# A three-stage kernel: the first chunk's scores from unspread blocks, a wake product, and a divided ordering of the experts

## The chip, the core and the metric

The kernel runs on one core of one Trainium2 chip. A core has TensorE (matrix products, PE in the rows), VectorE (DVE), ScalarE (ACT), GpSimd (POOL) and SyncE (SP, which here issues the loads), and 16 DMA engines that they share. The metric is the device time of the core in microseconds, the median of the runs.

## The reference

```python
q, k, a_re, a_im: [4, 8, 768, 48];  v the same;  all float32

for t in range(768):                                   # per batch and head
    ar, ai = normalised a_re, a_im at t                # a * min(|a|, 0.999) / (|a| + 1e-6)
    S_re, S_im = ar*S_re - ai*S_im + k[t] (x) v[t],  ar*S_im + ai*S_re
    y[t] = q[t] @ S_re
x = y as [3072, 384]                                   # tokens x (heads * 48)
xn = x / rms(x) * rms_g
h = silu(xn @ w_gate) * (xn @ w_val)                   # 384 -> 1536
x = h @ w_out                                          # 1536 -> 384
e = argmax(x @ w_gate2);  p = softmax at e             # 8 experts
out = p * (max(x @ w1[e], 0) @ w2[e])                  # 384 -> 1024 -> 384
```

The scan over t is done in closed form by chunks of 128 tokens: with the running product of a written as magnitude times phase, a chunk's scores are products of q times that running product and k divided by it, and a state of 48 x 48 per head goes from chunk to chunk.

## The kernel before

**Tiling.** The 3072 tokens are 12 units of 256 (two chunks of 128 each). A unit goes through three stages. *Elementwise* (`elem`, L485 to L627): magnitude, running products, phase, cosine and sine on tiles of 128 x 768 (three blocks j of 128 rows, which are heads times 48, by 256 tokens), on ScalarE and VectorE; the results are `qk` (q and k times the cosine) and `ee` (q and k times the sine). Ten DMAs then *spread* them (L625) from 128 rows, where a head of 48 lies across blocks, to `QK`, 96 rows (48 of cosine, 48 of sine) for each of 8 heads. *Attention* (`chunk`, L649): scores k q (L680), transposed k (L698), products with v (L720, and L724 with the state), transposition of the new state (L747) and of the rows (L765), norm, and transposition of the normed row y to x (L805). *Dense* (`feature`, L838): twelve features of 128 columns; the products into both gates (L850, 18 of 256 columns, split into high and low parts), tanh and products on ScalarE and VectorE, the rounding `hh` and its remainder `hl` (L867), and the output products (L873). The experts come last (`expert`, L1242): products L1299, rounding `ehh` and remainder `ehl` (L1308), products L1317.

**Weights.** The dense weights come as bfloat16 halves and are put together in the start (`convert`, L381): a memset on GpSimd, `top` (L395), `join` (L401), `high` (L408), and `low`, the remainder, which for two groups (`w000`, `wo00`) is made by products on TensorE (L430 and L431). `logit_columns` (L441) multiplies the output weights with the gate of the experts, transposing them first (L450), then L460 and the transposition L466. An expert's two weight matrices are loaded in 3 pieces of 1024 columns and 4 of 768 (`load_weights`, L1073), through one staging buffer `rawa` for the first expert and three buffers `rawb` for the others; ScalarE converts each piece (L1095) and VectorE or GpSimd takes the remainder.

**The order.** Nothing is written in the order in which it runs. Every step is added to a plan with its engines, costs, readers and writers and a due time, and `issue` (L185) puts them out: the step that can start first, by the plan's costs, and of an engine's equals the one that is due first. Due times come from a table of numbers (`TUNE`, L34). Each engine runs its own list in that order, and waits by semaphores.

**Fillers.** `keep_warm` (L1388) is a step of eight products of 128 x 384, whose result nobody reads. Fifteen such steps are added with a due time of 1e6, the last of all, so `issue` takes one where TensorE by its plan would wait; after 107.43 us of the plan they are left out.

**Ordering of the experts.** Beside the last dense features, VectorE sorts the experts by their counts in tiny operations: `second` (L1004, 7 operations) and `sort` (L1015, 8 operations), one step of the plan each.

## Time and profile before

| | us |
|---|---|
| median of 3 runs (935.48 to 936.58) | 936.08 |
| the profiled execution | 936.97 |
| its span, first to last instruction | 935.3 |
| TensorE busy | 896.5 (96%) |
| VectorE busy | 613.2 (66%) |
| ScalarE busy | 518.0 (55%) |
| GpSimd busy | 181.6 (19%) |

The span is that of the profiled execution, 1.7 us shorter than its time; the rest lies around it. Busy times are sums of one engine's instructions, and engines overlap.

### The profile page before, as it was taken

How to read it: one execution, taken by the hardware profiler on the slowest of the kernel's cores; microseconds unless marked ns; L12 is line 12 of the kernel's file. 1: busy time of each engine (PE TensorE's matmuls, PEld its weight loads, DVE VectorE, ACT ScalarE, POOL GpSimd, SP SyncE). 2: the span in 40 equal slices, each digit the busy share in tenths (PEclk: the TensorE clock that was granted, in tenths of full speed). 3: DMA queues.
4: the chain of work that ended last, by engine and by line, in shares of the span. 5: the costliest groups of instructions: out<-in, count | busy, mean ns of one | idle time of the engine just before them, and what ended most of it. 6: DMA issues, size and time to landing. Idle time of an engine off the chain costs nothing.

```text
span 935.3 us, 17743 instructions
## 1 busy us (share of the span) xinstructions
PE 896.5 (96%) x6747; PEld 863.5 (92%) x6747; DVE 613.2 (66%) x1528; ACT 518.0 (55%) x996; POOL 181.6 (19%) x226
## 2 busy tenths in 40 slices
PE   2699999999999999999999999999999999999996
PEld 2689999999999999999999999999989989999996
DVE  5699867778777768686868777546566642545510
ACT  7787876675655656655656565424426433544421
POOL 3232302010111010110201020101242532222121
PEclk9899999999999999999999999999999999999999
DMA  9955233423333140605050421102346753545200
GB/s 331 292 196 140 65 78 82 102 83 77 95 61 94 45 127 18 154 18 154 17 137 19 92 80 40 48 1 66 93 122 200 219 144 111 151 129 182 91 23 23
DMA packets 68363, 98.12 MB, mean 105 GB/s; under 512 B 16038, under 2 KB 49257, under 8 KB 68276
## 3 DMA queue, kind: packets, MB, share of 16 engines
q1 hardware_dynamic: 57316, 86.61, 32.9%
q0 software_dynamic: 10688, 9.95, 3.9%
q8 instruction: 54, 0.88, 0.4%
q10 hardware_dynamic: 272, 0.40, 0.1%
q14 instruction: 33, 0.27, 0.1%
HBM read 68.19 MB, written 10.15 MB: 84 GB/s over the span
## 4 chain that ended last, share of the span: by engine, by line
PE 68%; DVE 11%; issue 8%; DMA 5%; ACT 5%; POOL 2%; SPq 0%; POOLq 0%; DVEq 0%; ACTq 0%
PE m L850 25%; PE a L873 15%; PE a L1317 7%; PE m L1299 7%; PE t L680 4%; PE t L720 3%; DVE ee L541 2%; PE t L724 1%; DMA out_dram<-eo,idx 1%; PE t L698 1%; POOL out_dram L1325 1%; DMA QK<-qk 1%; DMA rawb<-in_w_dram 1%; DVE re L576 1%; DVE rs L785 1%
## 5 line engine op out<-in xcount | busy, mean ns | idle before, releaser
L850 PE MATMUL m<-xh,w 128*128 128x256 f32 x1728 | 276.6, 285 | 1.1 <-DVE s L862 0.6
L850 PEld LDWEIGHTS m<-xh,w 128*128 128x128 f32 x1728 | 234.6, 188 | 5.7 <-issue 3.4
L873 PE MATMUL a<-wo,hh 128*128 128x392 f32 (+1 forms) x576 | 151.8, 345 | 0.0
L850 PE MATMUL m<-xl,w 128*128 128x256 f32 x864 | 149.1, 281 | 0.0
L850 PEld LDWEIGHTS m<-xl,w 128*128 128x128 f32 x864 | 122.3, 188 | 0.0
L873 PEld LDWEIGHTS a<-wo,hh 128*128 128x128 f32 x576 | 100.5, 188 | 0.7 <-issue 0.7
L873 PE MATMUL a<-wo,hl 128*128 128x392 f32 (+1 forms) x288 | 98.3, 341 | 1.7 <-DVE hl L867 1.7
L865 ACT ACTIVATE hh<-s 128x256 fp32r<-128x256 f32 x144 | 59.5, 415 | 72.9 <-PE a L873 45.7
L857 ACT ACTIVATE s<-m 128x256 f32<-128x256 f32 x144 | 54.6, 380 | 77.8 <-PE m L850 40.1
L867 DVE TENSOR_TENSOR hl<-s,hh 128x256 fp32r<-128x256 f32 x144 | 66.6, 467 | 29.4 <-ACT hh L865 28.7
L859 DVE SCALAR_TENSOR_TENSOR s<-s,m 128x256 f32<-128x256 f32 x144 | 59.4, 413 | 21.3 <-ACT s L857 21.1
L1325 POOL DMA_INDIRECT out_dram<-eo,idx x28 | 37.2, 1330 | 157.7 <-ACT eo L1323 91.2
L1308 DVE SCALAR_TENSOR_TENSOR ehl<-m,ehh 128x384 fp32r<-128x384 f32 (+6 forms) x64 | 35.2, 555 | 44.6 <-ACT ehh L1306 44.0
L862 DVE SCALAR_TENSOR_TENSOR s<-s,m 128x256 f32<-128x256 f32 x144 | 59.6, 415 | 2.1
L1323 ACT ACTIVATE eo<-a,eg 114x384 f32<-114x384 f32 (+5 forms) x28 | 16.3, 582 | 74.9 <-PE a L1317 60.6
L873 PEld LDWEIGHTS a<-wo,hl 128*128 128x128 f32 x288 | 54.1, 188 | 2.3 <-DVE hl L867 2.3
L1306 ACT ACTIVATE ehh<-m 128x384 fp32r<-128x384 f32 (+6 forms) x64 | 31.2, 491 | 44.8 <-PE m L1299 41.7
L720 PE MATMUL t<-AK,vt 128*64 128x224 f32 (+3 forms) x384 | 49.6, 346 | 0.5 <-ACT raw L465 0.3
L680 PE MATMUL t<-QK 96*128 96x128 f32 x384 | 48.1, 276 | 0.3 <-DMA QK<-ee 0.3
L680 PEld LDWEIGHTS t<-QK 96*128 96x128 f32 x384 | 46.3, 192 | 1.3 <-issue 0.8
L948 POOL DMA_INDIRECT slots<-tid,sl x24 | 25.0, 1043 | 115.7 <-DVE cnt L943 111.8
L690 DVE TENSOR_TENSOR AK<-t,mask 128x512 f32<-128x512 f32 x40 | 26.9, 686 | 21.3 <-PE t L680 21.1
...
## 6 DMA issues: line engine op xcount, KB each, us to landing
...
```

The costliest lines, as they stand in the source:

```text
L680: TE.matmul(sc.t[:, i, :], lhsT=K(4 * g + i), rhs=Q(4 * g + i), start=True, stop=True)
L720: TE.matmul(yt.t[64 * n:64 * n + d, i, :n_], lhsT=vs[:, o:o + d], rhs=ak.t[:, 2 * i + n, :n_], start=True, stop=first)
L850: TE.matmul(ps.t[:, i, :], lhsT=W1[i, g].t[:, k, part, fs], rhs=x.t[:, k, :], start=(n == 0), stop=(n == 3 * KD - 1))
L857: add((A, act(U)), lambda e: e.activation(s.t, ps.t[:, 0, :], AF.Tanh, scale=0.5), r=[ps], w=[s], due=dh, table=AF.Tanh)
L859: add((V, dve(U)), lambda e: e.scalar_tensor_tensor(out=s.t, in0=s.t, scalar=1.0, in1=ps.t[:, 0, :], op0=ALU.add, op1=ALU.mult), r=[s, ps] ...
L862: add((V, dve(U)), lambda e: e.scalar_tensor_tensor(out=s.t, in0=s.t, scalar=0.5, in1=ps.t[:, 1, :], op0=ALU.mult, op1=ALU.mult), r=[s, ps ...
L865: add((A, act(U)), lambda e: e.activation(hh.t, s.t, AF.Copy), r=[s], w=[hh], due=dh)
L867: lambda e: e.tensor_tensor(out=hl.t, in0=s.t, in1=hh.t, op=ALU.subtract), r=[s, hh], w=[hl], due=dh, lock=True)
L873: TE.matmul(acc[t].t[:, :wide], lhsT=h.t[:, ts_], rhs=WO[g].t[:, k3, part, :wide], start=(f == 0 and n == 0), stop=(f == KF - 1 and n == 2))
L1299: TE.matmul(ps.t, lhsT=w.t[:, k, fs], rhs=y.t[:, k, :], start=(i == 0), stop=(i == 3 * KD - 1))
L1317: TE.matmul(po.t, lhsT=h.t[:, f, js], rhs=w.t[:, f, :], start=(f == 0 and i == 0), stop=(f == KF2 - 1 and i == 2))
L1325: add((G, 1.05), lambda e, o=o, j=j: e.indirect_dma_start(out=outs[(x + j) % len(outs)], out_offset=bass.IndirectOffsetOnAxis(ap=at(j), ax ...
```

## The change

**Scores of the first chunk.** They are no longer computed from `QK`, but from `qk` and `ee` as they stand in 128 rows, ahead of the spread. A head of 48 rows can start only at certain rows of a product's operand; so where another head's rows are in the way, the k side is a copy in which those are zero (`own`, by the column `part`). That takes 20 products instead of 8, each pair for cosine and sine. `rows` is split in two: the half with the scores needs no `QK`, the half for the state does and gets a later due time (`KS`).

```diff
+        def bank(*shape, own=True):
+            return Buf(k_u if apart and own else k_t, shape=list(shape))
...
                 out=S2.t, in0=T.t, in1=gm.t.unsqueeze(2).to_broadcast([2 * D, H, D]), op=ALU.mult),
                r=[T, gm], w=[S2], lock=True)
...
+        def places(h):
+
+            if h < 6:
+                return [(h // 2, slice(0, D) if h % 2 == 0 else slice(0, 2 * D), h % 2)]
+            return [(2 * (h - 6), slice(2 * D, P), 0), (1, slice(2 * D, 112 if h == 6 else P), h - 6)]
+
...
+                        TE.matmul(sc.t[:, i, :], lhsT=K(h), rhs=Q(h), start=True, stop=True)
+                        continue
+                    ops = [(pair[n].t[rs, j, U:U + C] if not masked else own.t[rs, n, j], pair[n].t[rs, j, :C])
+                           for n in range(2) for j, rs, masked in places(h)]
+                    for n, (k_, q_) in enumerate(ops):
```

(The lines above are the places of heads 6 and 7 and the products; `pair` is `qk` and `ee`.)

**Elementwise of the first unit.** Each operation is cut into two halves of 384 elements (one for each chunk), and the arctangent moves ahead of the exponentials. The steps of the first unit are marked `first`; `foresee` works out when each could start, and `issue` takes no other step on an engine that would run past that by over 0.1 us (`RS`), TensorE left out.

```diff
+    def foresee(self, firsts):
+
+        for s in firsts:
+            e, c = s.engs[0][:2]
+            t = s.span[0]
+            for d in s.deps:
+                t = max(t, (d.end if d.end is not None else d.done if d.first else math.inf)
+                        + self.hop(d.eng if d.end is not None else d.engs[0][0], e))
+            s.soon, s.done = t, t + c + s.lag + s.size / 350e3
...
                 raise RuntimeError("no step can be issued")
+            if firsts:
+                taken = {}
+                for s in firsts:
+                    e = s.engs[0][0]
+                    if e is not self.pe:
+                        taken[e] = min(taken.get(e, math.inf), s.soon)
+                cand = [c for c in cand if c[1].first or c[3] <= taken.get(c[2], math.inf) + TUNE["RS"]] or cand
...
+        parts = range(NC) if u == 0 else [None]
+        NE_ = N3 // len(parts)
+
+        def at(*a, shift=0.0, **kw):
+            due[0] += 1.0 / len(parts)
+            return add(*a, due=due[0] + shift, pull=(TUNE["PE0"], TUNE["PE1"])[u] if u < 2 else 0.0, first=u == 0, **kw)
...
+        order = [(0, 0), (1, 0), (0, 1), (1, 1)]
+        for i, sin in order:
+            key, y = "pm"[i], angle if sin else ta
+            each(either, lambda e, c, i=i, sin=sin, y=y: e.tensor_tensor(
+                out=half(ee if sin else qk, i, c), in0=half(ee, i, c), in1=cut(y, c), op=ALU.mult),
+                r=[(ee, key), y], w=[(ee, key) if sin else (qk, "qk"[i])], lock=True, shift=sh)
+        state["whole"] = qk, ee
+        state["moves"] = [] if u == 0 else state["moves"]
```

**Weight conversions.** Loads from the fourth conversion on wait for the last spread DMA; `top` runs on ScalarE or GpSimd only; the memset waits for the loads.

**Wake and warm-up.** TensorE's first instruction becomes a product that reads the first half of the exponential; behind it stand nine steps of eight products of 128 x 128 (`FE`), to be taken as fillers are.

```diff
 
         for k in range(KD):
             dma(lambda e, k=k: e.dma_start(halves()[:, k, 1:1 + 4 * WB], src[k * P:(k + 1) * P]),
-                P * WB * 8, w=[(st, f"k{k}")], due=due, after=paces[-AHEAD:][:1] if len(paces) >= AHEAD else ())
+                P * WB * 8, w=[(st, f"k{k}")], due=due, after=(paces[-AHEAD:][:1] if len(paces) >= AHEAD else [])
+                + (state["moves"][-1:] if len(paces) >= TUNE["NB"] else []))
         light = [(A, act(N)), (G, 0.08 + N * 1.04e-3), (V, dve(N / 2), TUNE["RB"])]
         pairs = [(st, f"k{k}") for k in range(KD)]
-        add((G, 0.08 + N * 0.96e-3), lambda e: e.memset(raw.t, 0.0), w=[raw], due=due - 2, lock=True)
-        paces.append(add(light, top, r=pairs, w=[raw], due=due, lock=True))
+        add((G, 0.08 + N * 0.96e-3), lambda e: e.memset(raw.t, 0.0), r=pairs[:1] if len(paces) > 1 else [], w=[raw], due=due - 2)
+        paces.append(add([(A, 0.16 + N * 1.11e-3), (G, 0.16 + N * 1.13e-3)], top, r=pairs, w=[raw], due=due, lock=True))
...
+    def wake(ee):
+        add((TE, mm(P, 4)), lambda e: TE.matmul(fill.t[:, :P], lhsT=ident, rhs=ee.t[:, 0, U:U + C], start=True, stop=True),
+            r=[(ee, "m0")], w=[fill], due=-2000.0)
...
+        def warm_up(e):
+            for _ in range(8):
+                TE.matmul(fill.t[:, :P], lhsT=identr, rhs=identr, start=True, stop=True)
+
+        for _ in range(int(TUNE["FE"])):
+            add((TE, 8 * 0.1125), warm_up, r=[IDENTR, fill], w=[fill], due=1e6, span=(0.0, TUNE["W1"]))
```

**Experts.** The sort is cut into `sort`, `ranked` and `numbered`, one step each. `rawa` has three buffers of 392 columns instead of one of 1024. The first expert's pieces are 9 of 384 or 256 columns and 8 of 384 (instead of 3 and 4); the last 768-column piece of the others from the third on is cut in two, which go through `rawa`, and their loads are planned 6 us long instead of 2.

```diff
-    k_ra, k_rb = Slots(e_right, "rawa", [P, F2], F32), Slots(e_left, "rawb", [P, F2], F32, 3)
+    k_ra, k_rb = Slots(e_right, "rawa", [P, XW], F32, 3), Slots(e_left, "rawb", [P, F2], F32, 3)
...
+        def pieces():
+
+            for k in range(KD):
+                for lo, hi in ((0, F2),) if x else ((0, DM), (DM, 2 * DM), (2 * DM, F2)):
+                    yield 0, k, lo, hi, k
+            for f in range(0, KF2, 2):
+                for lo, hi in ((f, f + 2),) if x == 1 or x and f + 2 < KF2 else ((f, f + 1), (f + 1, f + 2)):
+                    yield 1, f // 2, lo, hi, f / 2 + 0.2 * (lo - f)
...
+            raw = Buf(k_rb if cols > DM else k_ra) if x else Buf(k_ra)
...
+            loads.setdefault(x, []).append(dma(load, P * cols * 4, w=[raw], due=due, after=after, lag=TUNE["DL"] if x < 2 else 6.0))
...
-                add((V, 1.3), second, r=[MORE, HOT], w=[PERM, SECOND], due=due_moe(u + 1, KF))
-                add((V, 2.0), sort, r=[MORE, HOT], w=[PERM], due=due_moe(u + 1, KF))
+                add((V, 1.1), second, r=[MORE, HOT], w=[PERM, SECOND], due=due_moe(u + 1, KF), lock=True)
+                for c, fn in ((0.6, sort), (0.72, ranked), (0.36, numbered)):
+                    add((V, c), fn, r=[MORE, HOT], w=[PERM], due=due_moe(u + 1, KF), lock=True)
```

Of the table of numbers 33 values change, and seven are new:

```diff
-            E3=785.18, CG=483.05, CO=263.88, LC=-203.35, NRAW=2, AHEAD=5, DH=547.2, FI=-16.42, RP=-1165.15, TOL=0,
+            E3=785.18, CG=-303.74, CO=-326.35, LC=-1082.81, NRAW=2, SH=169.53, NB=4, FE=9, RS=0.1, ATD=1, KS=-1056.86, PM=0.0, AHEAD=5, DH=547.2, FI=-16.42, RP=-1355.1, TOL=0,
```

**What moves in the lists.** TensorE's list at the head of the program, the last logit transposes (L450), a filler run and the first scores (L680) before:

```order
L450 MATMUL t_301<-identr,wo_268 128x128 x6
L450 MATMUL t_309<-identr,wo_268 128x128 x6
L450 MATMUL t_318<-identr,wo_268 128x128 x6
L1388 MATMUL a_244<-w_333,identr 128x384 x16
L680 MATMUL t_372<-QK_288 128x128 x4
L680 MATMUL t_384<-QK_288 128x128 x4
L698 MATMUL t_397<-ident,QK_288 128x96 x4
L698 MATMUL t_403<-ident,QK_288 128x96 x4
```

and of after (the scores are L805 there, the fillers and the warm-ups L1556 and L1560, the wake product L515):

```order
L1728 UNCONDITIONAL_BRANCH
L515 MATMUL a_227<-ee_197,ident 128x128
L1560 MATMUL a_227<-identr 128x128 x64
L805 MATMUL m_328<-qk_146 128x128
L805 MATMUL m_328<-ee_197 128x128
L805 MATMUL m_328<-qk_146,tb_302 128x128
L805 MATMUL m_328<-ee_197,tb_302 128x128
L805 MATMUL m_328<-qk_146 128x128
L805 MATMUL m_328<-ee_197 128x128
```

All weight products, logit transposes and fillers that stood ahead of the first scores now stand behind them.

TensorE's list inside the first unit's dense features (L850 before, L983 after; `w100` and the like are weight groups: first the matrix, 0 the gate's and 1 the value's, then which 384 of the 1536 columns), before:

```order
L850 MATMUL m2_716<-xh0_565,w100_333 128x256 x3
L850 MATMUL m2_716<-xl0_587,w100_333 128x256 x3
L850 MATMUL m2_716<-xh0_565,w100_333 128x256 x3
L1388 MATMUL a0_244<-w020_743,identr_64 128x384 x16
L850 MATMUL m0_780<-xh0_565,w010_527 128x256 x3
L850 MATMUL m0_780<-xl0_587,w010_527 128x256 x3
L850 MATMUL m0_780<-xh0_565,w010_527 128x256 x3
L850 MATMUL m0_780<-xh0_565,w110_421 128x256 x3
```

and after:

```order
L983 MATMUL m1_826<-xh0_537,w010_543 128x256 x3
L983 MATMUL m1_826<-xh0_537,w110_707 128x256 x3
L983 MATMUL m1_826<-xl0_549,w110_707 128x256 x3
L983 MATMUL m1_826<-xh0_537,w110_707 128x256 x3
L1556 MATMUL a0_227<-w010_543,identr_64 128x384 x16
L1556 MATMUL a0_227<-w110_707,identr_64 128x384 x16
L983 MATMUL m0_915<-xh0_537,w010_543 128x256 x3
L983 MATMUL m0_915<-xl0_549,w010_543 128x256 x3
```

Where one run of 16 fillers stood between two features, 32 stand now, one feature later.

VectorE's list at the ordering of the experts, beside the last dense features (`hl` is L867 before, L1000 after), before:

```order
L1013 TENSOR_SCALAR half1_78<-piece_76 128x1
L1020 SCALAR_TENSOR_TENSOR upto_73<-hot_67,nk_68 1x8
L1023 TENSOR_TENSOR grid_69<-upto_73 1x64
L1024 TENSOR_REDUCE rank8_75<-grid_69 1x8
L1025 TENSOR_TENSOR grid_69<-rank8_75,rev_95 1x64
L1026 TENSOR_TENSOR grid_69<-grid_69,rev_95 1x64
L1027 TENSOR_REDUCE perm_70<-grid_69 1x8
L1028 TENSOR_SCALAR perm_70<-perm_70 1x8
L1029 CAST permi_71<-perm_70 1x8
L867 TENSOR_TENSOR hl2_8543<-s0_8406,hh2_8507 128x256
L867 TENSOR_TENSOR hl0_8555<-s1_8444,hh0_8516 128x256
L867 TENSOR_TENSOR hl1_8565<-s2_8480,hh1_8529 128x256
```

and after:

```order
L1146 TENSOR_SCALAR half1_78<-piece_76 128x1
L1000 TENSOR_TENSOR hl2_8718<-s0_8617,hh2_8700 128x256
L1153 SCALAR_TENSOR_TENSOR upto_73<-hot_67,nk_68 1x8
L1155 TENSOR_TENSOR grid_69<-upto_73 1x64
L1156 TENSOR_REDUCE rank8_75<-grid_69 1x8
L1000 TENSOR_TENSOR hl0_8733<-s1_8649,hh0_8716 128x256
L1163 TENSOR_TENSOR grid_69<-rank8_75,rev_95 1x64
L1164 TENSOR_TENSOR grid_69<-grid_69,rev_95 1x64
L1165 TENSOR_REDUCE perm_70<-grid_69 1x8
L1000 TENSOR_TENSOR hl1_8744<-s2_8682,hh1_8731 128x256
L1170 TENSOR_SCALAR perm_70<-perm_70 1x8
L1171 CAST permi_71<-perm_70 1x8
```

The three `hl` that stood behind all of the ordering now stand between its parts.

## Rows read from the trace of the kernel before

**Rows 1.** stretches: us, busy us (x instructions) per engine, granted clock, DMA share, GB/s

```profile
0.00:66.44 66.44, 41.38 (x269) 35.16 (x270) 45.71 (x81) 51.64 (x74) 22.11 (x51) 0.95 0.88 288
...
86.88:650.00 563.12, 560.42 (x4668) 541.53 (x4668) 413.94 (x1124) 333.03 (x684) 74.97 (x106) 1.00 0.30 75
```

**Rows 2.** what TensorE waited for from 66.44 us on: us in total, times, longest

```profile
PE m L1299 <- DVE ehl L1308: 1.8, 1, 1.8
PE a L873 <- DVE hl L867: 1.7, 1, 1.7
```

**Rows 3.** stretches of the fillers alone (L1388), the third row around their slow run

```profile
0.00:66.44 66.44, 19.67 (x96) 18.00 (x96) 0.95 0.88 288
66.44:83.73 17.29, 4.64 (x25) 4.11 (x24) 1.00 0.29 92
...
34.00:40.00 6.00, 3.09 (x10) 3.09 (x11) 0.50 1.07 165
```

**Rows 4.** timeline: start, us, instruction, [idle before <- releaser]; ScalarE, then VectorE

```profile
13.80 1.49 ACT L395 ACTIVATE raw<-w 128x1152 f16<-128x1152 bf16 x1 [2.24 <-DMA w<-in_wg_dram]
...
27.86 1.83 DVE L608 TENSOR_TENSOR qk<-ee,ta 128x768 f32<-128x768 f32 x2 [1.50 <-ACT ta L597]
...
50.29 0.55 DVE L704 COPY AK<-t 128x384 f32<-128x384 f32 x1
```

**Rows 5.** timeline of SyncE's queue (SPq), which issues the loads and the spread

```profile
29.75 3.04 SPq L625 DMA_DIRECT2D QK<-qk  x3
```

**Rows 6.** timeline of TensorE, from the second group's weight products on

```profile
27.95 0.81 PE L430 MATMUL t<-raw,ident 128*128 128x384 f32 x2
...
29.58 2.12 PE L450 MATMUL t<-identr,wo 128*128 128x128 f32 x18
36.91 4.59 PE L1388 MATMUL a<-w,identr 128*128 128x384 f32 x16 [5.21 <-ACT w L406]
41.34 0.39 PE L680 MATMUL t<-QK 96*128 96x128 f32 x2
42.01 1.80 PE L680 MATMUL t<-QK 96*128 96x128 f32 x14 [0.28 <-DMA QK<-ee]
...
45.75 1.06 PE L680 MATMUL t<-QK 96*128 96x128 f32 x8
...
51.66 0.85 PE L460 MATMUL t<-raw,w2gt 128*32 128x128 f32 x18
...
60.42 0.25 PE L466 MATMUL t<-ident,raw 96*128 96x96 f32 x1
60.45 3.02 PE L1388 MATMUL a<-w,identr 128*128 128x384 f32 x16
63.31 0.49 PE L805 MATMUL t<-ident,y 128*128 128x128 f32 x3
...
66.44 0.52 PE L850 MATMUL m<-xh,w 128*128 128x256 f32 x3
```

**Rows 7.** timeline of VectorE (two middle subtractions), then of GpSimd (one conversion)

```profile
16.60 2.03 DVE L554 TENSOR_TENSOR ee<-ee 128x256 f32<-128x256 f32 x3
...
66.19 1.09 DVE L554 TENSOR_TENSOR ee<-ee 128x256 f32<-128x256 f32 x3
...
16.76 1.27 POOL L408 TENSOR_SCALAR w<-raw 128x1152 fp32r<-128x1152 f32 x1 [7.58 <-DVE raw L401]
```

**Rows 8.** timeline at the experts' ordering: VectorE, then TensorE

```profile
675.08 1.41 DVE L1006 SCALAR_TENSOR_TENSOR upto<-hot,nk 128x8 f32<-128x8 f32 x1
...
679.31 1.08 DVE L867 TENSOR_TENSOR hl<-s,hh 128x256 fp32r<-128x256 f32 x3
...
679.77 0.44 PE L873 MATMUL a<-wo,hl 128*128 128x392 f32 x1 [1.66 <-DVE hl L867]
```

**Rows 9.** timeline in the experts: ScalarE, then TensorE

```profile
767.61 0.84 ACT L1095 ACTIVATE h2b<-rawb 128x768 fp32r<-128x768 f32 x1 [4.40 <-DMA rawb<-in_w_dram]
...
770.04 0.92 PE L1299 MATMUL m<-exh,h1a 128*128 128x456 f32 x3 [1.82 <-DVE ehl L1308]
```

434 lines of the change are left out of this document (261 added, 173 removed).

## The prediction, made before the result was known

> **What bounds the kernel now.** I read the stretches first: up to 66.44 us, the start of the first dense product, TensorE is busy for 41.4 of 66.4 us; from 86.88 to 650 us for 560.4 of 563.1 [rows 1]. So the kernel is a start of 66 us followed by 860 us that are TensorE's own. The list of what TensorE waited for after the start says the same: 1.8 us and 1.7 us in one wait each, and 2.0 us in four small ones left out there [rows 2]. Two rules follow. Whatever brings the first dense product forward shortens the run one to one; whatever is put into TensorE's order behind that point lengthens it one to one, unless it stands where the engine would have waited. The filler products (x128x384, they compute nothing that is used) are the second kind: of 120, 96 stand ahead of 66.44 us and 24 behind [rows 3].
>
> **The start, what is ahead of the spread.** The order of work is a chain: exponentials and sine on ScalarE, products on VectorE, the spread of q and k into 96 rows by ten DMAs, then attention of two chunks, then the first dense product. Before, the two q products follow the cosine from 27.86 to 29.69 us, and the first spread is issued at 29.75 [rows 4, 5]. On ScalarE two weight conversions of 1.5 us stand ahead of the exponentials of the chain, one of them shown [rows 4]; of the four table loads of that stretch none is saved. The change moves the conversions behind the exponentials (one stays, where ScalarE waits for VectorE) and cuts every operation in two halves, so that the second half of one step lies beside the first half of the next. I walk the new order with the old durations: an operation of 768 elements starts the next one 0.75 us later on ScalarE and 0.87 on VectorE, one of 384 elements 0.40 and 0.45 (the 384-wide copy has 0.55 us from start to end [rows 4]). Logarithms end at 8.0, the exponential table at 9.3, the four halves of inverse and magnitude at 10.9, arctan with its table at 13.1, the table back at 14.35; VectorE's scans end at 13.35, middle subtraction of the first half 15.1, the exponentials 17.0; phase, turns and subtraction on VectorE 19.4, absolute value 19.8, sine table 21.05, first cosine half 21.7; then eight half products of 0.45, the sixth of which completes q and k: 24.5 us. The spread thus starts at 24.6 instead of 29.75, 5.1 us earlier.
>
> **The start, from the spread to the dense product.** The last piece landed 12.3 us after the first issue (42.01) [rows 5, 6]. The loads queued ahead fall from 28 of 384 KB to 18, so the queue is empty when the spread comes, and I take 11.2; the first four DMAs, three quarters of the bytes, serve heads 0 to 3 and should land at 24.6 + 8.3 = 32.9. TensorE gets there from the other side: the first exponential half of k is ready at 16.7, the wake product and 64 warm-ups at the lower and then the higher clock end near 25.6, the 20 direct score products at 0.25 each (four heads in 1.06, ends overlapping [rows 6]) near 30.6, three weight products 2.4 and the first rows 0.5: 33.5. Both ends meet there, so neither alone is the bound. Then TensorE's order up to the first dense product is a fixed list. Before, the like list ran from the first score at 41.34 to 66.44, 25.1 us [rows 6], with 56 fillers and 1.5 us of waits; the new one has 56 fillers too. It loses the waits, chunk 0's scores (2.0), the logit product and its transposition (0.85 and 0.25) and, by my estimate, 1.2 on rows that read 128 or 96 columns where they read 224; it gains three weight products (0.81 each, 2.4), the logit transposes (2.1) and eight warm-ups (0.9, as eight of those 18), which ran earlier or not at all [rows 6]: 24.7 us. The first dense product comes at 33.5 + 24.7 = 58.2, a gain of **8.2 us**. I walked ScalarE and VectorE too: they have its operands at 55.6. The clock is no term: the 1.2 GHz level was granted from 34 to 40 us (0.50) [rows 3], after 5.2 us in which TensorE stood idle, and it fell on fillers (16 in 4.59 [rows 6]). In the new order no such pause stands there.
>
> **What is put behind the dense start.** 64 fillers instead of 24 now stand there: 40 x 0.179 (16 take 2.86, from 60.45 to 63.31 [rows 6]) = **+7.2 us**. They are put where the planner saw TensorE wait for VectorE (a free accumulator, then the third weight group). By my walk they overshoot those waits by 1.7 and 2.2 us, so fillers, not VectorE, set the pace there. The first logit product and its transposition, before ahead of the dense start, come behind it: **+1.1 us** (nine products and one transposition [rows 6]). The twelve extra score products, the split rows and the masked copies of q and k lie ahead of 58 us and are in the sums above. So the whole start costs 7.2 + 1.1 - 8.2 = 0.1 us: the 8 us gained at the first dense product are handed back as filler.
>
> **The experts' ordering.** At 675.08 us VectorE runs 14 tiny operations in one piece, the first of them 1.41 us, and the three hl products that TensorE waits for come behind, at 679.31; TensorE stood idle 1.66 us [rows 8]. The change puts one hl behind each of three parts. After the first part (2.6 us) the first hl is done at 678.0, and TensorE was free at 678.1; each next one comes 1.1 us later, as long as TensorE takes for one hl. I take **-1.5 us** of 1.66, the ends being 0 and -1.66.
>
> **The last weight piece of an expert.** At 767.61 ScalarE had sat 4.4 us before a conversion whose load was late, and three ehh operations were queued behind it in its order; TensorE lost 1.82 us [rows 9]. Now the last two pieces of each expert from the third on have staging buffers of their own (free since the first expert), and the load is planned 6 instead of 2 us long. Ends 0 and -1.82; no later load stalled TensorE, so I take **-1.8**. The smaller pieces of the first expert (16 loads instead of 7) run where TensorE waits for nothing [rows 2] and cost nothing while that cover lasts; without it each is one more wait of the order of 0.5 us. The other waits (2.0 us in sum) I leave as they are.
>
> **Sum.** 0.1 - 1.5 - 1.8 = -3.2 us. The profiled execution took 936.97 us (span 935.3), so 933.8; the median 936.08 lies 0.9 below it, so **932.9 us**.
>
> **A rule that speaks against it.** VectorE's middle subtraction took 2.03 us with a GpSimd conversion running beside it (16.76 to 18.03) and 1.09 us without [rows 7]. The change gives GpSimd four more top conversions (1.5 us each, as on ScalarE [rows 4]) and three more high ones (1.27 [rows 7]) in the start, some 10 us more of such work beside VectorE operations that read two tiles. The Trainium skill, SBUF — State Buffer, section "Who interferes with whom", says that a VectorE instruction with two SBUF inputs contends with a GpSimd instruction that reads SBUF, and the loser blocks for the whole instruction. By that rule the trace's pair is as it should be, and the sum would lose what the fourth rival below loses.
>
> **Rivals.** (1) *More than that*: the walk has slack (operands at 55.6), the second and third hl wait nothing, and the 2.0 us of small waits go with the new order: 1.2 + 2.0 + 0.2 more, 929.5. For it: these waits hang on single placements [rows 2]. Against: any new order makes new ones. Chance 0.14. (2) *The stalls move*: the hl after the second part or another late load stops TensorE for as long as before: the sum is 0.1, 936.2. For it: VectorE is the engine that both waited for. Chance 0.14. (3) *The spread lands late*: heads 0 to 3 arrive only with the rest, as at 41 us before (first score at 41.34, but TensorE was busy with fillers up to then [rows 6], so the trace does not say); the list starts at 36.3, dense at 61, +2.8: 935.7. Chance 0.08. (4) *GpSimd blocks VectorE*, the one on the other side: 10 us of GpSimd work at up to its whole length, of which 3.9 us are covered by the filler overshoot. At 0.74 us lost per us (0.94 for 1.27 [rows 7]) 7.4 - 3.9 = +3.5, no change in sum; at the whole length +6.1, 939.0. It decides from 9.0 us lost: then the run is slower by over 0.2%. For it: rows 7. Against: the planner keeps most of these apart. Chance 0.12. The forecast itself has 0.52, from 931 to 934.2.
>
> **Chances and range.** A difference under 0.2% (1.9 us) can't be told from none here. Faster: forecast and (1), 0.66; same: (2) and (3), 0.22; slower 0.12. The dense start can be off by 1 to 4 us (57 to 62) and the two stalls by 3.3, so the range is 928.5 to 937.5; it leaves out most of (4) and the tail of (1).
>
> **What would show it.** The first spread issued near 24.6 us, the first dense product near 58, TensorE's granted clock never at its lower level after 22 us; 64 fillers behind the dense start with no wait longer than 0.3 us ahead of 88 us; no wait of TensorE for hl beside the ordering, none for ehl in the experts. If the first dense product comes after 61.5, or TensorE waits behind the fillers, the start is wrong; if the time falls by over 8 us, fillers were standing in waits that I took for work.

## The result, and the profile after

The changed kernel takes 950.24 us (median of 4 runs, 949.58 to 952.13) against 936.33 (935.48 to 938.17) for the kernel before beside it: a ratio of 1.0142, 95% interval 1.012 to 1.0164. It is slower by 13 to 14 us; 932.9 was predicted, with a range up to 937.5. The profiled execution took 949.58 us, 12.61 more than that of before.

Three points cut both kernels into the same three parts: the first dense product, the first product of the experts, and the end of the span. The first row is before, the last one is what the prediction's terms make of it.

| profiled execution | to the first dense product | dense stages | experts | span |
|---|---|---|---|---|
| before | 66.44 | 617.39 | 251.47 | 935.3 |
| after | 73.61 | 626.05 | 248.04 | 947.7 |
| difference | +7.17 | +8.66 | -3.43 | +12.4 |
| predicted | -8.2 | +6.8 | -1.8 | -3.2 |

(+6.8 is 7.2 of fillers, 1.1 of logit products, -1.5 of the ordering, which lies ahead of the experts' first product.) So the late part did better than predicted, the dense stages are 1.9 us worse, and the start is wrong by 15.4 us and in its sign.

The first view to read is the list of what TensorE waited for in the kernel after (us in total, times, longest):

```profile
PE a L515 <- POOL qk L655: 17.2, 1, 17.2
PE m L983 <- DVE s L995: 2.4, 3, 1.8
...
PE a L1006 <- DVE hl L1000: 0.6, 1, 0.6
```

The 17.2 us are the idle time ahead of its first instruction, the wake product. Behind that there are no 12 us of waits: TensorE was never idle for long, so the time must lie in how long its instructions take. The timeline of TensorE in the start of the kernel after (start, us, instruction, number):

```profile
17.19 0.77 PE L515 MATMUL a<-ee,ident 128*128 128x128 f32 x2 [17.19 <-POOL qk L655]
17.61 13.89 PE L1560 MATMUL a<-identr 128*128 128x128 f32 x64
31.43 0.79 PE L805 MATMUL m<-qk 48*128 48x128 f32 x2
...
42.04 1.65 PE L456 MATMUL t<-raw,ident 128*128 128x384 f32 x2
42.91 1.09 PE L457 MATMUL t<-w,x 128*128 128x384 f32 x1
...
46.11 0.75 PE L457 MATMUL t<-w,x 128*128 128x384 f32 x1
46.79 0.65 PE L847 MATMUL m<-AK,vt 128*64 128x128 f32 x8
...
49.69 1.09 PE L1560 MATMUL a<-identr 128*128 128x128 f32 x8
...
73.61 0.52 PE L983 MATMUL m<-xh,w 128*128 128x256 f32 x3
```

Compare the two L1560 rows: eight warm-ups take 1.09 us at 49.69 (0.14 each, pipelined ends included), and 64 of them take 13.89 us at 17.61 (0.217 each). The weight pair (L456 here, L430 in [rows 6]) takes 1.65 us where it took 0.81. Up to about 46 us TensorE ran at the lower of its two levels (1.2 GHz, against 2.4 at the upper one). The stretches of that time (us; busy us and instructions of PE, PE's weight loads, DVE, ACT, POOL; granted clock; DMA share; GB/s) do not say so:

```profile
17.19:31.43 14.24, 14.24 (x66) 14.12 (x66) 10.73 (x20) 8.36 (x13) 1.94 (x2) 1.00 0.58 177
31.43:42.04 10.61, 10.61 (x41) 9.04 (x41) 1.96 (x2) 1.16 (x1) 0.00 (x0) 1.00 0.88 237
42.04:46.79 4.75, 4.75 (x10) 2.82 (x9) 1.96 (x2) 0.49 (x1) 1.09 (x2) 1.00 1.05 387
```

The clock column (1.00 for the upper level, 0.50 for the lower) reads 1.00 in all three. It was the same in the kernel before, with 1.00 from 16.7 to 21 us although its first weight pair took twice as long as the third:

```profile
16.73 1.65 PE L430 MATMUL t<-raw,ident 128*128 128x384 f32 x2 [16.73 <-DVE raw L401]
...
20.01 0.81 PE L430 MATMUL t<-raw,ident 128*128 128x384 f32 x2
```

In these traces the column shows a fall that follows a rise [rows 3], not the level at which the program begins. That level is to be read from the duration of one and the same instruction at two places.

Elsewhere: GpSimd's conversion stood beside two VectorE operations as the fourth rival had it, the spread was issued at 26.59 instead of 24.6, and no wait for `hl` stands at the ordering nor one for `ehl` in the experts (a wait of 0.6 us for `hl` lies at 142.7 us, in another unit). SyncE's queue, VectorE and GpSimd of the kernel after:

```profile
26.59 1.40 SPq L719 DMA_DIRECT2D QK<-qk  x2
```

```profile
18.76 2.25 DVE L684 TENSOR_TENSOR im<-re,ta 128x384 f32<-128x384 f32 x2
18.86 1.81 POOL L422 TENSOR_SCALAR raw<-w 128x1152 f16<-128x1152 bf16 x1 [1.54 <-DMA w<-in_wv_dram]
```

### The profile page after: what moved, and what is told of

It is laid out like the page before. It is cut to its first block, busy times and chain, and to the rows that moved or that the text cites. A ratio compares the mean times of both kernels' runs of the same rounds, so it can differ in the third digit from the quotient of the medians.

```text
span 947.7 us, 18182 instructions
## 1 busy us (share of the span) xinstructions
PE 917.9 (97%) x6877; PEld 883.3 (93%) x6877; DVE 622.6 (66%) x1564; ACT 516.0 (54%) x1026; POOL 182.1 (19%) x234
## 4 chain that ended last, share of the span: by engine, by line
PE 71%; DVE 9%; issue 8%; ACT 5%; DMA 5%; POOL 1%; SPq 0%; POOLq 0%; DVEq 0%; ACTq 0%
PE m L983 24%; PE a L1006 14%; PE m L1465 8%; PE a L1483 7%; PE t L800 4%; PE t L847 3%; PE a L1560 2%; PE t L851 1%; DMA rawa<-in_w_dram 1%; DMA out_dram<-eo,idx 1%; DVE ee L600 1%; PE m L805 1%; PE t L823 1%; DVE re L663 1%; POOL out_dram L1491 1%
## 5 line engine op out<-in xcount | busy, mean ns | idle before, releaser
L983 PE MATMUL m<-xh,w 128*128 128x256 f32 x1728 | 276.3, 285 | 2.6 <-DVE s L995 2.4
L983 PEld LDWEIGHTS m<-xh,w 128*128 128x128 f32 x1728 | 234.0, 188 | 7.7 <-DVE s L995 4.3
L983 PE MATMUL m<-xl,w 128*128 128x256 f32 x864 | 148.8, 281 | 0.0
L983 PEld LDWEIGHTS m<-xl,w 128*128 128x128 f32 x864 | 122.0, 188 | 0.0
L1000 DVE TENSOR_TENSOR hl<-s,hh 128x256 fp32r<-128x256 f32 x144 | 63.8, 448 | 24.0 <-ACT hh L998 23.1
L847 PE MATMUL t<-AK,vt 128*48 128x224 f32 (+5 forms) x384 | 47.7, 337 | 0.6 <-ACT AK L827 0.3
L800 PE MATMUL t<-QK 96*128 96x128 f32 x352 | 44.8, 277 | 0.0
L800 PEld LDWEIGHTS t<-QK 96*128 96x128 f32 x352 | 42.6, 191 | 1.0 <-issue 1.0
L815 DVE TENSOR_TENSOR AK<-t,mask 128x512 f32<-128x512 f32 x40 | 27.1, 686 | 17.2 <-PE t L800 17.1
```

The costliest lines, as they stand in the source:

```text
L800: TE.matmul(sc.t[:, i, :], lhsT=K(h), rhs=Q(h), start=True, stop=True)
L847: TE.matmul(yt.t[64 * n:64 * n + d, i, :], lhsT=vs[:, o:o + d], rhs=ak.t[:, 2 * i + n, lo:hi], start=True, stop=first or lo > 0)
L983: TE.matmul(ps.t[:, i, :], lhsT=W1[i, g].t[:, k, part, fs], rhs=x.t[:, k, :], start=(n == 0), stop=(n == 3 * KD - 1))
L1000: lambda e: e.tensor_tensor(out=hl.t, in0=s.t, in1=hh.t, op=ALU.subtract), r=[s, hh], w=[hl], due=dh, lock=True)
```

## Experiments

Two questions: why was TensorE at the lower level for the first 30 us of its work, and what is the change worth without that? The first theory is that the *shape* of the new warm-ups (128 columns, each with a weight load of its own, instead of 384 columns) does not bring the level up in this kernel; its rivals are that the time goes elsewhere whatever the level, and that the new scores themselves are at fault. Each expectation names its own theories by letters. Edits are against the kernel after unless said otherwise; times are medians, "before" the kernel before on the same chip beside it.

**wide: the same warm-ups with 384 columns.**

```diff
-            for _ in range(8):
-                TE.matmul(fill.t[:, :P], lhsT=identr, rhs=identr, start=True, stop=True)
+            for _ in range(5):
+                TE.matmul(fill.t.rearrange("p (k n) -> p k n", k=KD), lhsT=identr,
+                          rhs=identr.unsqueeze(1).to_broadcast([P, KD, P]), start=True, stop=True)
```

> The changed kernel, with each of the nine warm-up steps as five products of 128x384 instead of eight of 128x128; every other instruction and its order are as they were. Theory A (width): TensorE ran at its lower level from 17.2 to 46 us because nothing but products of 128 columns ran there; 384-wide ones bring it to the upper level some 4 us after 17.2, as the 384-wide weight products did in the kernel before (16.73 to 20.8). Then the 40 products end near 27, the first chunk's scores take 5.3 instead of 10.6 us and the three weight products 2.4 instead of 4.75: first dense product at 60 to 64 instead of 73.6, run 937 to 940. Theory B (not the width: the level rises about 29 us after the first product, whatever runs): 40 products at 0.36 take 14.4, as long as the 64 did, and the run stays at 949 to 951.

942.55 us (940.19 to 944.65) against 937.65; ratio 1.0051 (1.0028 to 1.0074). The first dense product comes at 64.94 us, 8.7 earlier. That is theory A, with both of its numbers missed by a little (60 to 64, 937 to 940). TensorE's timeline in wide, and the stretch at its end:

```profile
17.62 8.83 PE L1560 MATMUL a<-identr 128*128 128x384 f32 x40
26.38 0.49 PE L805 MATMUL m<-qk 48*128 48x128 f32 x2
...
32.85 1.65 PE L456 MATMUL t<-raw,ident 128*128 128x384 f32 x2
```

```profile
21.60:26.38 4.78, 4.78 (x28) 4.53 (x27) 4.78 (x11) 3.32 (x8) 0.00 (x0) 1.00 0.09 29
26.38:31.40 5.02, 5.02 (x35) 4.29 (x35) 3.49 (x4) 1.52 (x2) 0.00 (x0) 1.00 0.81 168
31.40:37.95 6.55, 6.55 (x17) 4.05 (x17) 1.96 (x2) 1.29 (x2) 1.25 (x2) 0.50 0.87 212
```

Of the 40 products 13 begin in the 4.0 us up to 21.6 and the other 27 in the 4.8 behind: the level rises some 4 us after the first of them, and the score pairs take 0.49 instead of 0.79. Then, five microseconds into the scores, it *falls*: the column now shows 0.50, and the weight pairs take 1.65 again. So the shape of the warm-ups was the cause of the low level, and the scores do not keep the upper one. Yet wide is still slower than before.

**nowarm: no warm-ups at all.**

```diff
         def warm_up(e):
-            for _ in range(8):
-                TE.matmul(fill.t[:, :P], lhsT=identr, rhs=identr, start=True, stop=True)
+            return
```

> The changed kernel with the warm-up products left out (the wake product stays), all else in its order. Theory A (width): the scores start when q and k are ready, at 26.5 instead of 31.4, still at the lower level, since they too are 128 columns wide; 10.6 us of scores and 4.75 of weight products as in the changed kernel: first dense product near 68.7, run 945. Theory B (the warm-ups themselves hold the level down): the scores take 5.3 us, first dense product 61 to 63, run 937 to 939.

948.71 us (948.19 to 951.91), ratio 1.0124 (1.0104 to 1.0145). TensorE's timeline in nowarm:

```profile
23.73 0.79 PE L805 MATMUL m<-qk 48*128 48x128 f32 x2 [5.90 <-DVE qk L705]
...
34.84 1.65 PE L456 MATMUL t<-raw,ident 128*128 128x384 f32 x2
```

The scores begin at 23.7, run at the lower level from the first to the last and do not raise it in 11 us. The dense start is at 66.84: the narrow warm-ups cost the kernel after 6.8 us there and bought nothing. The run got back only 1.5 of these. The lead over after is still whole, 6.8 us, at 185 us (the transposition of y, L938, at 185.02 against 191.78), and 2.3 us at 225. In between it was lost on a load: behind the spread of the fourth unit ScalarE sat 3.05 us for a load of a_re (0.73 in after), its copy `AK` was queued behind that, and TensorE waited for `AK` for 2.62 us (0.30 in after), with a granted clock of 0.83 in 210 to 220 us (1.00 in after). ScalarE, then TensorE, in nowarm:

```profile
212.32 0.84 ACT L577 ACTIVATE ta<-re 128x768 f32<-128x768 f32 x1 [3.05 <-DMA re<-in_a_re_dram]
```

```profile
213.60 0.97 PE L847 MATMUL t<-AK,vt 128*64 128x224 f32 x8 [2.62 <-ACT AK L827]
```

**raise and bnarrow: does a narrow product fail to raise the level, or to hold it?** raise has 384 columns in the first two warm-up steps alone; bnarrow is the kernel before with its first 24 fillers as 72 of 128 columns, at a place where the level is already up.

```diff
+            state["warm"] = state.get("warm", 0) + 1
+            if state["warm"] <= 2:
+                for _ in range(6):
+                    TE.matmul(fill.t.rearrange("p (k n) -> p k n", k=KD), lhsT=identr,
+                              rhs=identr.unsqueeze(1).to_broadcast([P, KD, P]), start=True, stop=True)
+                return
```

> The changed kernel with the first two of its warm-up steps as six products of 128x384 each (12 in all), the other seven as they are, eight of 128x128 each. Theory C (wide products raise the level, narrow ones hold it and do not raise it): 12 wide at 0.36 to 0.2 us until some 21.5, then 48 narrow at 0.11 to 0.13, 5 to 6 us, end near 27.5; the scores start at the upper level (0.32 each), first dense product near 66. Theory A (narrow products let the level fall): the narrow ones go over to 0.217 after some 5 us, end near 30, scores at 0.57, first dense product at 70 to 72. Theory D (operands: the identity times itself holds no level): the narrow ones at 0.217 from the start, end at 32.

```diff
+            state["fills"] = state.get("fills", 0) + 1
+            if state["fills"] <= 3:
+                for _ in range(3 * int(TUNE["FN"])):
+                    TE.matmul(fill.t[:, :P], lhsT=identr, rhs=w.t[:, k, 0, :P], start=True, stop=True)
+                return
```

> The kernel before, with the first 24 fillers (128x384, from 20.83 us) as 72 of 128x128, as many columns; all else in its order. Theory A (products of 128 columns let the level fall, wherever they stand): they begin at the upper level, at 0.126 each, and after about 5 us take 0.217, 12 us in all; the second group's weight products behind them run at the lower level (1.6 us each instead of 0.81). Theory B (only the start of the changed kernel keeps the level down): all 72 at 0.126, 9.1 us, the weight products at 0.81.

One execution each: raise 945.12 us, bnarrow 937.97. TensorE's timeline in raise, then in bnarrow:

```profile
17.19 4.19 PE L1562 MATMUL a<-identr 128*128 128x384 f32 x12
21.17 5.80 PE L1566 MATMUL a<-identr 128*128 128x128 f32 x48
26.90 0.48 PE L805 MATMUL m<-qk 48*128 48x128 f32 x2
...
32.69 0.63 PE L805 MATMUL m<-ee,tb 32*128 32x128 f32 x2
```

```profile
20.39 8.15 PE L1390 MATMUL a<-w,identr 128*128 128x128 f32 x72
28.37 0.86 PE L430 MATMUL t<-raw,ident 128*128 128x384 f32 x2
```

The very products that took 0.217 us each in after take 0.12 here, 48 of them in a row, once twelve wide ones have raised the level; in bnarrow 72 take 0.113 each, and the weight pair behind them is fast (0.86). "Narrow products keep the clock down" is therefore too simple: they did not *raise* the level in 13.9 us, but they *held* it for 5.8 and 8.2 us (theory C of raise, theory B of bnarrow). The scores of 32 to 96 rows did not hold it: in raise the level falls at about 32 us as in wide, and the dense start is at 65.43.

**mix, mix2, mix3, wide2: can the level be held through the scores?** mix is wide with one product of 384 columns behind each head's scores; mix2 and mix3 are the same kernel again, wide2 is wide again, one execution each.

```diff
                     for n, (k_, q_) in enumerate(ops):
...
+                    for _ in range(1):
+                        TE.matmul(fill.t.rearrange("p (k n) -> p k n", k=KD), lhsT=identr,
+                                  rhs=identr.unsqueeze(1).to_broadcast([P, KD, P]), start=True, stop=True)
```

> As wide, with one product of 128x384 (0.18 us at the upper level) behind each head of the first chunk's scores, eight in all. Theory A (products of 128 columns alone let the level fall): in wide it fell at 31.4 us, after 5 us of these scores, and the three weight products took 4.9 instead of 2.4. With the wide products between, the level stays: scores end near 33.5, weight products near 36 instead of 37.9, first dense product at 63 instead of 64.9, run 2 us under wide. Theory B (the level falls at that point for another reason): scores and weight products as slow as in wide and 1.4 us more: first dense product at 66.3, run 1.4 us above wide.

> The kernel of mix once more, for a second profile: its profiled execution took 939.53, the other four 943.6 to 948.0 with a lower mean granted clock (0.993 to 0.995 against 0.998). Theory A (a stretch at the lower level behind a late spread, as in wide_nolate from 208 to 217 us, comes in some executions and not in others): if this execution is over 943, its profile shows such a stretch of some 10 us with a wait for a spread ahead of it. Theory B: a longer start, no such stretch.

> The kernel of mix again, for a third profile; executions took 939.5 to 948.0. Theory A: if this one is over 943, its profile has a stretch of some 10 us at the lower level behind a late spread. Theory B: the difference lies in the start, first dense product 2 us or more later than 64.0.

> The kernel of wide again, for a second profile; wide's executions took 940.2 to 944.7. Theory A (a stretch at the lower level behind a late spread, as in wide_nolate from 208 to 217 us, comes in some executions): if this one is over 942, its profile has such a stretch. Theory B: the difference lies in the start, first dense product 2 us or more later than 64.9.

mix: 945.65 us (939.53 to 947.96), ratio 1.0096 (1.0061 to 1.013); its profiled execution is the fastest of its five. mix2 took 939.52, mix3 942.12, wide2 939.18. The first weight pair behind the scores in mix, and the second one in mix2:

```profile
34.58 0.81 PE L456 MATMUL t<-raw,ident 128*128 128x384 f32 x2
```

```profile
34.92 1.48 PE L456 MATMUL t<-raw,ident 128*128 128x384 f32 x2
```

In mix the level was held through the weight products, in mix2 and mix3 it fell at about 33.5, so the wide ones between the scores are not to be relied on, and neither theory of mix fits all three. Holding the level buys little: dense start 63.99, 64.53, 64.54 against 64.94 and 64.44 in wide and wide2. Why other executions of mix and wide take up to 948 and 945 is only partly known. One place is seen: mix3 has a wait of 1.5 us for `AK` at 209.85 us, raise one of 2.2 us at 211.28 with the clock at 0.91 in the 20 us around it, where wide2 has none. It is the place of nowarm's wait, and the same load: ScalarE sat 1.92 us for it in mix3, 2.64 in raise and 0.34 in wide2. Why it lands later in some executions is open, and the slowest executions themselves were not profiled (mix2, mix3 and wide2 all stayed under the times at which their theories would have been tested).

**wide_nolate and wide_nofill: are the fillers behind the dense start the 7.2 us that they seem?** wide, without the 64 fillers behind the dense start, and without any fillers.

```diff
-            for _ in range(int(TUNE["FN"])):
+            state["fills"] = state.get("fills", 0) + 1
+            for _ in range(int(TUNE["FN"]) if state["fills"] <= 7 else 0):
```

> As wide, and without the 64 fillers behind the start of the dense products (32, 24 and 8 of 128x384; 11.2 us of TensorE in the changed kernel). By the prediction's walk they overshoot the waits for VectorE that they fill by 3.9 us: 3 to 4 us less than wide, with waits of 7 to 8 us in their place. If fillers stood in waits throughout: as wide. If VectorE and ScalarE were never late there: 11 us less than wide.

> As wide, without any of the 120 fillers, those 56 ahead of the dense start (10 us) too. If the fillers ahead of it stand in waits for the spread, ScalarE and VectorE, the dense start stays where wide has it, and the run is that of wide_nolate; as far as they set the pace it comes up to 10 us earlier. If the pauses bring the lower level back, the products around them take up to twice as long and it is slower than wide_nolate.

(wide_nofill has `False` in place of the comparison with 7.) wide_nolate 948.06 us (947.09 to 948.4), ratio 1.0109 (1.0094 to 1.0124): 5.5 us *slower* than wide, which none of the three cases had. wide_nofill 940.83 (940.26 to 943.94), ratio 1.004 (1.002 to 1.006), with the dense start at 61.72. The waits of TensorE in wide_nolate:

```profile
PE m L983 <- DVE s L995: 7.6, 5, 4.9
PE t L476 <- DVE wo L436: 2.6, 1, 2.6
...
PE m L983 <- DVE w L436: 1.2, 1, 1.2
```

The stretch that held the 64 fillers, in wide and in wide_nolate, and a later one of wide_nolate:

```profile
66.00:92.00 26.00, 26.00 (x204) 25.46 (x203) 22.43 (x40) 19.58 (x34) 8.96 (x9) 1.00 0.18 62
```

```profile
66.00:92.00 26.00, 19.90 (x153) 18.95 (x152) 23.08 (x40) 19.57 (x33) 8.12 (x9) 0.87 0.13 46
...
210.00:220.00 10.00, 8.37 (x50) 7.46 (x51) 4.80 (x12) 6.45 (x9) 0.00 (x0) 0.66 0.22 74
```

Without its fillers TensorE waits for VectorE in their place, for `s`, for the logit weights `wo` and for the weight group `w`, and falls to the lower level for a while (0.87). The first output product comes at 91.45 us instead of 94.40, but at 110 us wide_nolate is only 0.85 ahead, of which 0.82 were there at the dense start. It is VectorE, busy 22 to 23 of these 26 us, that sets the pace: its order runs on at the same distance from the dense start, with or without the fillers (the second unit's q product at 90.25 in wide and at 89.41 in wide_nolate, 0.84 earlier). wide_nofill says it again: a dense start 3.2 us earlier than wide's, but the q product at 89.89 and the first output product at 91.94, no earlier than in wide_nolate. In these runs the fillers were not work added to the path, but waits with a cover on. What made wide_nolate slower lies later, at the load that nowarm lost its lead on: wide_nolate is 0.9 us ahead of wide at 182 us and 5.4 behind at 224. The load is issued at 202.0 in both, but ScalarE sat 4.07 us for it against 0.58, TensorE waited 1.4 us for `QK` and 2.0 for `AK`, and the lower level followed (0.66). wide_nofill waited only 0.5 us for `AK` there.

**indirect: the spread scores back, everything else as in wide.**

```diff
-        direct, apart = u == 0 and c == 0, u == 0
+        direct, apart = False, u == 0
```

> As wide, with the first chunk's scores from the spread blocks again, as in the kernel before; the plan orders the start anew, everything else of the change is in. Theory A (scores ahead of the spread bring the list forward, as the prediction has it, and the level is a matter of its own): TensorE has no scores to do before about 37 us, the list starts some 3 us later than in wide: first dense product at 67 to 68 instead of 64.9, run 3 us above wide. Theory B (their 5 us of 128-column products cost as much by the level as they bring): first dense product at 63 to 65.5, run within 1 us of wide.

963.26 us (960.7 to 966.11), ratio 1.0268 (1.0234 to 1.0302), dense start 66.47. The planner put out another order, with waits of 6.8, 5.7 and 4.4 us (the last in six pieces) that wide does not have, so the run decides between neither theory, and what the direct scores alone are worth stays open. Only that TensorE read the spread's first heads at 34.7 to 35.4 us is of use below.

**sort1: the ordering in one piece again.**

```diff
-                add((V, 1.1), second, r=[MORE, HOT], w=[PERM, SECOND], due=due_moe(u + 1, KF), lock=True)
+                add((V, 1.1), lambda e: [f(e) for f in (second, sort, ranked, numbered)], r=[MORE, HOT], w=[PERM, SECOND], due=due_moe(u + 1, KF), lock=True)
...
-                    add((V, c), fn, r=[MORE, HOT], w=[PERM], due=due_moe(u + 1, KF), lock=True)
+                    add((V, c), lambda e: None, r=[MORE, HOT], w=[PERM], due=due_moe(u + 1, KF), lock=True)
```

> The changed kernel with the ordering of the experts in one piece again (second, sort, ranked and numbered in a row, the three hl behind them), all else in its order. Theory A (the division took TensorE's wait away): the wait for hl of 1.66 us comes back, run 1.5 us above the changed kernel. Theory B (TensorE would have waited for something else there): no wait for hl over 0.5 us, run as the changed kernel.

952.02 us (951.12 to 955.17), ratio 1.0165 (1.0128 to 1.0202); span 949.2 instead of 947.7. The waits in sort1:

```profile
PE m L983 <- DVE s L995: 3.0, 3, 2.4
PE a L1006 <- DVE hl L1000: 1.7, 2, 1.1
```

A wait for `hl` of 1.1 us is back at the ordering, beside the one of 0.6 that after has too: that is what the division is worth in after. The wait for `s` also grew by 0.6, but it ends at 686.20, ahead of the ordering, which begins at 693. The rest of the 1.66 us of before goes with another difference: the first tiny operation, 1.41 us in [rows 8], ran there beside a subtraction on GpSimd, and takes 0.17 in after and in sort1, where GpSimd does nothing at that time. GpSimd in before:

```profile
674.63 1.84 POOL L1099 TENSOR_TENSOR l2a<-rawa,h2a 128x768 fp32r<-128x768 f32 x1 [12.05 <-ACT h2a L1095]
```

The intervals of sort1 and after overlap; it is the wait that speaks, not the medians.

**whole0, late, late3, late3lag: the late parts by themselves.** In after a wait of 1.80 us at 685.71 came back. ScalarE and TensorE there:

```profile
682.36 0.52 ACT L1249 ACTIVATE h2a<-rawa 128x384 fp32r<-128x384 f32 x1 [3.40 <-DMA rawa<-in_w_dram]
```

```profile
685.71 0.62 PE L983 MATMUL m<-xh,w 128*128 128x256 f32 x3 [1.80 <-DVE s L995]
```

It is the wait of [rows 9] in another place: ScalarE's conversion of a first expert's piece sits 3.4 us for its load, the `s` of a feature is queued behind it, and TensorE stops. whole0 makes the first expert's pieces whole again in after (one `rawa` of 1024 columns). late is the kernel before with the divided ordering, the first expert's pieces whole, the later experts' last pieces cut and the longer planned load; late3 the kernel before with all late parts exactly as in after; late3lag late3 with the first expert's loads planned 6 us long too.

```diff
-    k_ra, k_rb = Slots(e_right, "rawa", [P, XW], F32, 3), Slots(e_left, "rawb", [P, F2], F32, 3)
+    k_ra, k_rb = Slots(e_right, "rawa", [P, F2], F32), Slots(e_left, "rawb", [P, F2], F32, 3)
...
-                for lo, hi in ((0, F2),) if x else ((0, DM), (DM, 2 * DM), (2 * DM, F2)):
+                for lo, hi in ((0, F2),):
...
```

> The changed kernel, with the first expert's weights in 7 whole pieces through one staging buffer of 1024 columns again (instead of 17 through three of 392); the last pieces of the later experts stay cut in two and go through that buffer; loads stay planned 6 us long. Theory A (the small pieces are late one after the other, and ScalarE's tanh for TensorE waits behind a conversion of them): TensorE's wait of 1.80 us at 685.71 goes, run 1.8 us under the changed kernel; the wait for ehl, 1.82 us in the kernel before, stays away. Theory B (that wait comes from where the loads stand, not from their size): it stays or moves, run within 0.5 us of the changed kernel.

> The kernel before, with the divided ordering of the experts, the cut last pieces of the later experts (through the single staging buffer of 1024) and loads planned 6 us long, and nothing else of the change: the start and the first expert's pieces are those of before. Theory A (these parts take 1.66 and 1.82 us of waits away and cost nothing): 3.3 us under the kernel before. Theory B (the waits come back elsewhere, as one did at 685.71 in the changed kernel): within 1 us of the kernel before.

late3's edit of the kernel before is the change's own part on the experts, word for word; late3lag differs from it in one line:

```diff
-lag=TUNE["DL"] if x < 2 else 6.0
+lag=TUNE["DL"] if x == 1 else 6.0
```

> The kernel before, with the whole of the change behind the dense stages and nothing ahead of them: the ordering of the experts divided, three staging buffers of 392 columns, the first expert's weights in 17 pieces, the cut last pieces of the later experts, loads planned 6 us long. Theory A (in the changed kernel these took 1.66 and 1.82 us of waits away and brought one of 1.80, in the first expert's pieces): 1.7 us under the kernel before if that wait comes here too, 3.3 if not. Theory B (without the small buffers' place in the changed order the waits come back): a wait for ehl or hl of over 1.5 us, within 0.5 us of the kernel before or above it.

> As late3, with the first expert's loads planned 6 us long too (2 in late3, where ScalarE stood up to 3.9 us before a conversion of such a piece with tanh queued behind it). Theory A (the plan puts a conversion ahead of tanh because it expects its load too early): TensorE's wait of 1.8 us for the features goes, 1.8 us under late3. Theory B (three small buffers are simply too slow for 17 loads): a wait of about that size stays, or the first expert starts late; run within 0.7 us of late3 or above it.

| kernel | us | ratio to before (95%) | longest late wait of TensorE |
|---|---|---|---|
| whole0 | 957.4 (956.3 to 958.67) | 1.0216 (1.0182 to 1.0249) | 3.5 for `ehl` |
| late | 940.23 (938.72 to 942.75) | 1.0032 (1.0016 to 1.0048) | 4.8 for `ehl` |
| late3 | 935.46 (932.76 to 936.99) | 0.9975 (0.9962 to 0.9989) | 1.8 for `s` |
| late3lag | 938.74 (937.04 to 939.8) | 1.0024 (1.0013 to 1.0034) | 3.9 for `ehl` |

The waits of late3, then of late3lag, and late3lag's stretch around its wait:

```profile
PE m L850 <- DVE s L862: 2.4, 3, 1.8
```

```profile
PE m L1332 <- DVE ehl L1341: 3.9, 1, 3.9
```

```profile
700.00:720.00 20.00, 16.15 (x115) 15.75 (x114) 13.38 (x33) 10.87 (x25) 5.11 (x3) 0.91 0.59 159
```

whole0 came out some 7 us above after and late 2.2 above before, which neither of their theories had; late3 is near theory A; in late3lag the wait for `s` went, as its theory A had it, and the longer one for `ehl` came.

late3 is the fastest kernel of this study, faster than both: 935.46 us against 937.46 beside it, and 247.81 us of experts in its profile. (Its first dense product, at 65.51, is earlier than before's, but its edit touches nothing ahead of that, and late3lag has 66.97.) The gain of the change lies here and is about a quarter of a per cent. The wait of 1.8 us for `s` belongs to the small pieces (it stands in late3 at 669.35 as in after at 685.71) and is the smaller evil: take it away, by whole pieces or by a longer planned load, and a wait of 3.5 to 4.8 us for `ehl` comes in the first expert, followed by the lower level.

## Why the prediction was wrong, by its own steps

**The start, TensorE's side: the step that failed.** "The wake product and 64 warm-ups at the lower and then the higher clock end near 25.6": they never reached the higher one. And "the clock is no term": it was the largest. Here is the walk to 58.2 beside what came; wide is the same order with the warm-ups' shape mended.

| step | predicted | after | error | wide | error |
|---|---|---|---|---|---|
| end of the warm-ups | 25.6 | 31.4 | +5.8 | 26.4 | +0.8 |
| scores | 5.0 | 10.6 | +5.6 | 6.5 | +1.5 |
| three weight products | 2.4 | 4.75 | +2.35 | 5.1 | +2.7 |
| first rows, then the list to the dense start | 25.2 | 26.8 | +1.6 | 27.0 | +1.8 |
| first dense product | 58.2 | 73.6 | +15.4 | 64.9 | +6.7 |

The weak point was there to see. [rows 6] priced the warm-ups by products that ran when the level was up, and looked for the lower level in the clock column, where before shows it at 34 to 40 us alone. The kernel before begins at the lower level too, on the pair of 1.65 us ahead of [rows 6]; what ran there until it rose were products of 384 columns, which the new order put behind the scores. None of the cases that the prediction weighed had a level that stays down.

The Trainium skill, "TensorE: Matmul & The Clock Gate", section "What you observe", tells of 64 products of 128 x 128 x 128 in bf16, one behind the other, that go over to the upper level on the way. Here 64 warm-ups of 128 columns (float32 tiles) did not, at 0.217 us each; by that page alone one would have forecast the step as I did, and the measurement decides. What the section "What's actually happening" says, that the lower level is the default and activity lifts it, wide agrees with (13 products begin in its first 4.0 us of warm-ups, 27 in the next 4.8).

Of the smaller errors, the scores took 0.32 each and not 0.25 even at the upper level: [rows 6] have pairs on 96 rows one behind another, the new ones change tile and rows each time. They also lose the level at their end, and the weight products behind them took 5.1 us where 2.4 were forecast.

**The start, the spread.** Issued at 26.59, 2.0 us late. Of these 1.2 are the fourth rival's: the two operations beside GpSimd's conversion took 2.25 us, and 1.01 in wide, where the conversion came later. It lay off the path, since TensorE came to the scores later than that. The rival's mechanism was right and its price, 3.5 to 6.1 us, was not paid. The third rival was wrong: in indirect TensorE read the first heads 8.1 to 8.8 us after the first issue at 26.62, as the 8.3 of the walk had it.

**Behind the dense start.** +7.2 for fillers and +1.1 for the logit products fit the size, but by luck: the dense stages of wide (690.60 - 64.94) are 8.3 us longer than before's, with the vanished wait of 1.66 and a new wait of 1.7 to 1.8 (below) in that sum. The reading under it was wrong. "Fillers, not VectorE, set the pace there": without them the same time passes in waits for VectorE, since the second unit's elementwise work now falls into that place. (Weight conversions do not fill it: VectorE makes 4 in these 26 us of wide, 7 in the same stretch of before.) The second unit's q product on VectorE, in before, wide and wide_nolate:

```profile
81.12 1.83 DVE L608 TENSOR_TENSOR qk<-ee,ta 128x768 f32<-128x768 f32 x2 [0.90 <-ACT ta L597]
```

```profile
90.25 2.53 DVE L705 TENSOR_TENSOR qk<-ee,ta 128x768 f32<-128x768 f32 x2 [0.39 <-ACT ta L692]
```

```profile
89.41 1.66 DVE L705 TENSOR_TENSOR qk<-ee,ta 128x768 f32<-128x768 f32 x1 [0.39 <-ACT ta L692]
```

It comes 14.7 us behind the first dense product in before and 25.3 behind it in wide.

The rule that whatever brings the first dense product forward shortens the run one to one needs a condition with that: the other engines must come forward too, and no load may be late. From after to wide they did: 8.7 us at the first dense product, 8.7 at the second unit's q product (98.91 and 90.25), 9.3 of span. In nowarm they did as well, and the 6.8 us were lost at 205 to 225 us on the load. In wide_nofill TensorE came 3.2 us forward alone, and by 126 us it was 2.8 behind wide (L938 at 126.11 against 123.30), after its waits and a granted clock of 0.87 in 66 to 92 and 0.81 in 92 to 110 us; that is the profiled execution, the slowest of its four, and the median lies 1.7 us under wide's, with ranges that overlap.

Even with the warm-ups mended, the start gains 1.5 us at the dense product and pays 8.3 behind it; the experts give 3.7 back (938.4 - 690.60 = 247.8), and the span is 3.1 us longer than before's. So with the warm-ups mended the change is still slower by about half a per cent (wide: 1.0051, with the fall of the level behind the scores in it); the level at the beginning makes it one and a half.

**The ordering.** -1.5, and right in the number: the wait of 1.66 us for `hl` is gone. The mechanism is right too, but worth 1.1 (sort1); the rest goes with the operation of 1.41 us that shrank to 0.17 without GpSimd beside it, which the prediction counted at full length in the first part's 2.6 us, so that much was luck. (The tiny operations are 15, not 14.) And 1.8 us came back in front of the experts by the first expert's small pieces (17, not 16), of which I had said that they cost nothing "while that cover lasts". The cover did not last there; that is about the +1.9 by which the dense stages missed.

**The last weight piece of an expert.** Right in kind and too small: -3.43 (late3: -3.66) instead of -1.8. The wait of 1.82 us in [rows 9] was followed by slow products, in the kernel before: the same triple of 456 columns ahead of the wait, behind it, and the stretch.

```profile
767.43 0.78 PE L1299 MATMUL m<-exh,l1a 128*128 128x456 f32 x3
...
771.90 1.34 PE L1299 MATMUL m<-exh,l1a 128*128 128x456 f32 x3
773.04 1.30 PE L1299 MATMUL m<-exh,h1a 128*128 128x456 f32 x3
```

```profile
770.00:780.00 10.00, 9.96 (x46) 9.28 (x47) 5.18 (x7) 4.10 (x6) 0.00 (x0) 0.83 0.26 57
```

Triples start 1.14 us apart there and 0.62 ahead; with three and a part of them slow, that is 0.10 + 3 x 0.52 = 1.7 us on top of the 1.82, 3.5 in all. Here the clock column does show it, as the level had been up before.

**The rivals.** None of the four named the mechanism. The one on the slower side was about VectorE and GpSimd; the one that was needed is "the new first work of TensorE leaves the level down", from 17.6 us on, priced by the pair of 1.65 us instead of 0.81 over the scores and weight products: 13.9 + 10.6 + 4.75 against 8 + 5 + 2.4.

**What stays open.** Why the second unit's elementwise work comes later behind the dense start than before; what the direct scores alone are worth (indirect has another order); whether the scores lose the level by their few rows or by another trait of theirs; what the executions of wide and mix at 944 to 948 us did, which were not profiled; why the load of a_re lands later in some executions; and what in the narrow warm-ups fails to raise the level.
